# Row groups for depth-2 products, a re-cut wq gradient pass and an earlier second pass in a one-token transformer block's backward kernel

## The chip, the core and the metric

The kernel runs on one core of a Trainium2 chip. The metric is the device time of one execution in microseconds, from launch to end, as the median of 13 runs. The profile is of one execution; its span is counted from the first to the last instruction of the core.

## The reference, cut to what matters

The reference is the forward and the backward pass of one pre-norm block for a single decoded token: two batch rows (B=2), width D=640, 32 heads of depth 128, a cache of 4096 keys and values for each head, and a ReLU MLP of width 1728. All tensors are bfloat16.

```
h  = x + softmax(LN(x) wq  K^T * scale) V  wo
h2 = h + relu(LN(h) w1) w2
out_0 = h2
out_1..out_7 = gradients of x, k_cache, v_cache, wq, wo, w1, w2 for grad_out
```

Nearly all bytes belong to the caches. The gradients of K and V (out_2, out_3) are 64 tiles of 1 MB each, one for each pair of batch row and head. The four weight gradients out_4 (wq), out_5 (wo), out_6 (w1) and out_7 (w2) are outer products summed over the two batch rows, so each is a matrix product whose contraction has depth 2. The gradient of x also needs wq once more: the gradient of q times the transpose of wq.

## The kernel before, in words

**First pass.** `p1_iter(i)` (L373) is a software pipeline over the 64 (row, head) pairs. For pair i it transposes the K tile on TensorE (L327), lets ScalarE or VectorE copy the transposed groups from PSUM (L332, L330) and forms the scores (L338). For pair i-1 it computes the exponentials and the scaled keys `pk` on VectorE (L388). For pair i-2 it runs the sums over V and K (L381, L396). Its result is, for each pair, a matrix MT, two columns in OU (L489) and the probabilities P_bf.

**Middle.** `middle_gen(b)` (L609) is one generator for each batch row. It forms attention output, layer norm, MLP, and the gradient back to the output of attention. `go_group` (L566) then gives, for eight heads at a time, the gradient goc of each head's output: eight VectorE reductions (`ttr`, L552), a pair of matmuls `pr_ps` (L265) whose result goes to gom, and the matmuls `d_ps` (L581, L584) from which negdot and GQc, the gradient of q, come. `mlp_out(b)` (L593) computes and stores the block's output.

**Second pass.** `p2_iter(j)` (L688) takes pair j: it loads the V tile again (called Wt), transposes it as fp32 pairs (L348), multiplies with gom (L361), gets gsp (L696), and writes gradient tiles gK and gV by VectorE (two halves each, L683). GpSimd queues their stores (L721, L740). gK and gV share three buffers, and seven `ld` buffers hold K, V, W and the tiles of the last part.

**Last part.** `fin_gen` (L786) runs in the second pass's shadow. `rows_of` (L747) turns columns into rows with one small matmul per 128 values (L754) and a ScalarE copy (L756). `outer_rows` (L762) forms a weight gradient: each depth-2 matmul (L778, at most 512 columns) goes to one of three PSUM banks (`mid`, `m`, `a`) in turn, ScalarE copies it to an `ot` tile (L780), and GpSimd queues the store (L783). After the wo gradient and after all heads' GQc it reads wq in five tiles of 8 KB rows (L809), transposes them in groups of eight (L327, L332), and sums 32 heads into `gx_ps` (L822), which VectorE copies for each of five column blocks (L825). `ln_bwd`, two row stores and the wq gradient follow.

**What sets the order.** The kernel schedules by hand. A plan lists iterations: first-pass iteration i, with a second-pass pair j in every other one from `P2_AT` on, then second-pass pairs alone. Between the pipeline's steps, generators in two lists are advanced (`bg_step`): the middle with a credit of RATES per step, the last part with RATE2 per step; each yield costs what it states. `wait(n)` holds a generator back for some steps, `turn()` hands out slots for `ttr`, and `bg_until` forces the middle on at once when a pair j needs a head group that isn't ready. Loads are queued on SyncE in the order of a list (`pump`), as buffers come free. On each engine instructions run in the order in which they were emitted.

Of the kernel before, what the change touches and what calls it, by code (L numbers as in the profile page):

```python
# [7 lines left out]
FP32 = mybir.dt.float32  # L8
BF16 = mybir.dt.bfloat16
ALU = mybir.AluOpType  # L10
# [5 lines left out]
def kernel(  # L16
# [533 lines left out]
    def ttr(in0, in1, acc, width, kc=128):  # L550
        junk = cols.tile([128, D], BF16, tag="junk", name="junk")
        nc.vector.tensor_tensor_reduce(out=junk[0:kc, 0:width], in0=in0, in1=in1, scale=1.0, scalar=0.0,  # L552
                                       op0=ALU.mult, op1=ALU.add, accum_out=acc)
# [9 lines left out]
    def one(src, b):  # L563
        return src[:, :, b]

    def go_group(b, g, hbc):  # L566

        hs = slice(g * GH, (g + 1) * GH)
        go32 = small.tile([128, GH], FP32, tag="go32", bufs=1, name="go32")
        for k in range(GH):  # L570
            yield from turn()
            ttr(wo_t[:, g * GH + k, :], hbc[:], go32[:, k:k + 1], D)
            yield 0.9
        nc.vector.tensor_copy(out=goc[:, hs, b], in_=go32[:])
        pr = small.tile([128, GH], FP32, tag="pr", bufs=1, name="pr")
        nc.vector.tensor_tensor(out=pr[:], in0=goc[:, hs, b], in1=OU[:, b, hs, 0], op=ALU.mult)
        yield from wait(3)
        pair_rows(gom, goc, hs, slice(b, b + 1))
        yield from wait(2)
        d_ps = pst([128, 2, GH], FP32, "mid", "d_ps")  # L580
        nc.tensor.matmul(d_ps[:, 0, :], lhsT=ones_f32, rhs=pr[:], start=True, stop=True)  # L581
        for k in range(GH):
            h = g * GH + k
            nc.tensor.matmul(d_ps[:, 1, k:k + 1], lhsT=MTs.pop((b, h))[:], rhs=goc[:, h, b:b + 1],  # L584
                             start=True, stop=True)
        nc.vector.tensor_scalar(out=negdot[:, hs, b], in0=d_ps[:, 0, :], scalar1=-1.0, scalar2=None, op0=ALU.mult)
        ud = small.tile([128, GH], FP32, tag="ud", bufs=1, name="ud")
        nc.vector.tensor_tensor(out=ud[:], in0=OU[:, b, hs, 1], in1=negdot[:, hs, b], op=ALU.mult)
        nc.vector.tensor_tensor(out=ud[:], in0=d_ps[:, 1, :], in1=ud[:], op=ALU.add)
        nc.vector.tensor_scalar(out=GQc[:, hs, b], in0=ud[:], scalar1=SCALE, scalar2=None, op0=ALU.mult)  # L590
        yield ("go", b, g)

    def mlp_out(b):  # L593
        m_ps = pst([128, ND], FP32, "mid", "mlp_ps")
# [14 lines left out]
    def middle_gen(b):  # L609
# [47 lines left out]
        hbc = cols.tile([128, D], BF16, tag="rowbc", name="hbc")  # L657
        yield from bcast_cols(one(gh1c, b), ND, lambda c: 128, hbc)
        yield ("gh1", b)
        yield from go_group(b, 0, hbc)  # L660
        if b == 0:
            yield from mlp_out(b)
        for g in range(1, H // GH):
            yield from go_group(b, g, hbc)

    def ga_gen():

# [76 lines left out]

    fw = [0]

    def rows_of(pool, colsrc, n, total, name, tag):  # L747

        r = pool.tile([B, n * 128], BF16, tag=tag, bufs=2 if tag == "rD" else 1, name=name)
        for c0 in range(0, n, 4):  # L750
            cn = min(4, n - c0)
            t = pst([B, 512], FP32, "mid", "rw_ps")
            for k in range(cn):
                nc.tensor.matmul(t[:, k * 128:(k + 1) * 128], lhsT=colsrc[:, c0 + k, :], rhs=ident_bf[:],  # L754
                                 start=True, stop=True)
            nc.scalar.copy(out=r[:, c0 * 128:(c0 + cn) * 128], in_=t[:, 0:cn * 128])  # L756
            yield
        FIN[name] = r

    FIN = {}  # L760

    def outer_rows(pool, L, nrow, R, N, out_ap, cc):  # L762

        P = nrow // cc
        grp = max(1, min(cc, 4096 // N))
        out_v = out_ap.rearrange("(p c) n -> p c n", c=cc)
        for c0 in range(0, cc, grp):
            gn = min(grp, cc - c0)
            while free["ld"] < 1:
                yield  # L770
            ot = take("ld", [128, grp, N], "ot")
            for k in range(gn):
                n0 = 0
                while n0 < N:
                    nn = min(512, N - n0)
                    fw[0] += 1
                    o_ps = pst([128, 512], FP32, ("mid", "m", "a")[fw[0] % 3], "o_ps")
                    nc.tensor.matmul(o_ps[0:P, 0:nn], lhsT=L[:, bass.ds(c0 + k, P, step=cc)], rhs=R[:, n0:n0 + nn],  # L778
                                     start=True, stop=True)
                    nc.scalar.copy(out=ot[0:P, k, n0:n0 + nn], in_=o_ps[0:P, 0:nn])  # L780
                    n0 += nn
                    yield 0.55
            nc.gpsimd.dma_start(out=out_v[:, c0:c0 + gn, :], in_=ot[0:P, 0:gn, :])  # L783
            give(ot)

    def fin_gen(fin):  # L786
        yield from rows_of(fin, acol, NF, Dff, "ar", "rF")
        yield from rows_of(fin, gc, ND, D, "gr", "rD")
        yield from outer_rows(fin, FIN["ar"], Dff, FIN["gr"], D, out_7, Dff // 96)
        yield from rows_of(fin, ghfc, NF, Dff, "ghfr", "rF")  # L790
        yield from rows_of(fin, x2c, ND, D, "x2r", "rD")
        yield from outer_rows(fin, FIN["x2r"], D, FIN["ghfr"], Dff, out_6, ND)
        while ("gh1", B - 1) not in done:
            yield
        yield from rows_of(fin, OFc, H, HD, "OFr", "rH")
        yield from rows_of(fin, gh1c, ND, D, "gh1r", "rD")
        yield from outer_rows(fin, FIN["OFr"], HD, FIN["gh1r"], D, out_5, HD // 128)
        while ("go", 1, H // GH - 1) not in done:
            yield
        gx1 = fin.tile([128, B, ND], FP32, tag="gx1", name="gx1")  # L800
        wqn = A_wq.rearrange("(c p) n -> p c n", p=128)
        nxt = None
        for c in range(-1, ND):
            st = nxt
            if c + 1 < ND:
                while free["ld"] < 1:
                    yield
                nxt = take("ld", [128, NSC, 128], "wqs")
                nc.sync.dma_start(out=nxt[:], in_=wqn[:, c + 1, :].rearrange("p (h n) -> p h n", n=128))  # L809
            if c < 0:  # L810
                for _ in range(8):
                    yield
                continue
            acc = pst([128, B], FP32, "m", "gx_ps")
            for g in range(H // GT):
                t_sb = transpose_group(st, g)
                if g == H // GT - 1:
                    give(st)
                yield 0.9
                for j in range(GT):  # L820
                    h = g * GT + j
                    nc.tensor.matmul(acc[:], lhsT=t_sb[:, j, :], rhs=GQc[:, h, :],  # L822
                                     start=(h == 0), stop=(h == H - 1))
                yield
            nc.vector.tensor_copy(out=gx1[:, :, c], in_=acc[:])  # L825
        gx_bf = fin.tile([128, ND, B], BF16, tag="gxb", name="gx_bf")
        yield from ln_bwd(gx1[:], x1c[:], rstd1[:], gh1c[:], gx_bf[:], B)
        for b in range(B):
            gxo = small.tile([128, ND], BF16, tag="gxo", bufs=2, name="gxo")
            nc.vector.tensor_copy(out=gxo[:], in_=gx_bf[:, :, b])  # L830
            store_row(gxo[:], ND, out_1[b].rearrange("s (c p) -> (s c) p", p=128))
            yield
        yield from rows_of(fin, GQc, H, HD, "GQr", "rH")
        yield from rows_of(fin, x1c, ND, D, "x1r", "rD")
        yield from outer_rows(fin, FIN["x1r"], D, FIN["GQr"], HD, out_4, ND)


    bg = []
# [32 lines left out]
            assert bg and bg_one(bg) >= 0.0, mark  # L871
        forced[0] = False

    M0_ITERS = 12
    P2_AT = H + 2 + M0_ITERS
    RATES = (0.2, 0.6, 0.2, 0.8, 0.45)
    RATE2 = 0.68
    plan = []
    i = j = 0
    while i <= NP1 + 1 or j <= NP1:  # L880
# [58 lines left out]
    for n, (i, j) in enumerate(plan):  # L939
# [5 lines left out]
        if j is not None:  # L945
            while g2 is not None:
                p2_step()
            if j < NP1:
                bg_until(("go", j // H, (j % H) // GH))
            g2 = p2_iter(j, int(i is not None))  # L950
        reserve[0] = 2 if bg2 else 0
        if i is None and ("y", 1) in done and fin is None:
# [19 lines left out]
        for k, _ in enumerate(p1_iter(i, i < H + 1, int(H + 1 < i < P2_AT))):  # L972
            for _ in range(at.get(k, 0)):
                if g2 is not None:
                    p2_step()
            if k == 5:
                a_heads(i)
            pump()

            spread[0] = 1 if i < P2_AT else 2  # L980
            if i >= P2_AT:
                slot[0] = int(k == 6)
            elif i > H + 1:
                slot[0] = {1: 2, 4: 1, 6: 1}.get(k, 0)
            else:
                slot[0] = int(k in (1, 6))
            bg_step(0, rate)
            bg_step(1, RATE2)
# [38 lines left out]
```

## Time and profile before

| what | value |
|---|---|
| median of 13 runs | 1041.45 us (1034.02 to 1047.33) |
| the profiled execution | 1045.12 us |
| its span, first to last instruction | 1043.3 us |
| mean granted TensorE clock | 0.751 of full speed |
| moved by DMA | 221.48 MB read, 149.13 MB written, 355 GB/s over the span |
| weight loads of TensorE (PEld) | 745.6 us busy, 71% |
| VectorE / ScalarE | 654.3 us (63%) / 586.0 us (56%) |

The profile's page gives busy times of the engines, the span in 40 slices (each digit is a busy share in tenths; PEclk is the granted TensorE clock in tenths; DMA is the mean busy share of the core's 16 DMA engines), the chain of work that ended last, and groups of equal instructions with the idle time of the engine before them. A table of stretches gives the same for chosen stretches of time. Matmul ends are modelled, so a busy PE isn't PE at its peak. A DMA share can read slightly over 1.

### The profile page before, as it was taken

The page shows a single profiled execution, that of the slowest core. Times are in us where ns is not written, and L with a number is a line of the kernel's source. Part 1 is how long each engine was busy: PE and PEld are TensorE (multiplying, and loading weights), DVE is VectorE, ACT ScalarE, POOL GpSimd, SP SyncE. Part 2 cuts the span into 40 slices and gives each one's busy share as a digit, 9 for nine tenths or more (in the row PEclk, how much of TensorE's full clock was granted, in tenths as well). Part 3 has the DMA queues.
Part 4 walks back from the last instruction along what each step waited for, and adds up shares of the span by engine and source line. Part 5 has one row for each costly group of instructions (what it writes and reads, how often), then busy time and mean ns, then how long its engine had stood idle before and what let it go on. Part 6 is the DMA issues. An engine that isn't in the chain of part 4 may idle for free.

```text
span 1043.3 us, 30344 instructions
## 1 busy us (share of the span) xinstructions
PE 853.8 (82%) x13231; PEld 745.6 (71%) x13231; DVE 654.3 (63%) x1252; ACT 586.0 (56%) x1227; POOL 102.9 (10%) x220
## 2 busy tenths in 40 slices
PE   6999999999999998889896659898996465738971
PEld 5999999998888888878785547655666355625661
DVE  3545867755476575656586668675775675563556
ACT  4666656667675666656553336665663244626741
POOL 1000000000000000000011212121121111111212
PEclk9989989989797888978886555555556666865565
DMA  9999999998576498989899998998999999987998
GB/s 357 379 391 407 384 367 383 379 369 317 202 263 227 165 389 337 352 336 369 358 383 426 382 371 321 344 368 333 411 423 411 426 362 384 417 351 286 390 412 348
DMA packets 59748, 372.56 MB, mean 357 GB/s; under 512 B 5760, under 2 KB 15424, under 8 KB 17376
## 3 DMA queue, kind: packets, MB, share of 16 engines
q1 hardware_dynamic: 38960, 221.50, 56.0%
q0 software_dynamic: 20656, 149.14, 34.5%
q8 instruction: 103, 1.69, 0.6%
q14 instruction: 29, 0.24, 0.1%
HBM read 221.48 MB, written 149.13 MB: 355 GB/s over the span
## 4 chain that ended last, share of the span: by engine, by line
PE 56%; DMA 21%; ACT 8%; DVE 8%; issue 5%; POOL 0%; SPq 0%; POOLq 0%; DVEq 0%; ACTq 0%
PE t_ps L327 12%; PE m_ps L381 11%; PE t_ps L348 10%; DMA out_dram<-gK 8%; DMA Kt<-in_A_k_cache_dram 6%; DMA out_dram<-gV 6%; PE o_ps L778 4%; PE m_ps L396 4%; ACT t_sb L332 4%; DVE gV L683 4%; PE s_ps L338 4%; PE dp_ps L361 2%; DVE gK L683 2%; PE t_ps L319 2%; PE rw_ps L754 1%
## 5 line engine op out<-in xcount | busy, mean ns | idle before, releaser
L332 ACT COPY t_sb<-t_ps 128x1024 bf16<-128x1024 bf16 x243 | 239.7, 1014 | 86.7 <-PE t_ps L327 85.0
L348 PE MATMUL t_ps<-ident_f,Wt 128*128 128x128 f32 x1024 | 236.3, 380 | 0.8 <-ACT t_sb L332 0.5
L353 ACT COPY t_sb<-t_ps 128x512 f32<-128x512 f32 x256 | 149.2, 586 | 150.2 <-PE t_ps L348 147.2
L381 PE MATMUL m_ps<-pk,Vt 128*128 128x129 bf16 x2048 | 208.9, 232 | 1.9 <-issue 1.9
L348 PEld LDWEIGHTS t_ps<-ident_f,Wt 128*128 128x128 f32 x1024 | 167.6, 196 | 38.7 <-issue 19.7
L388 DVE TENSOR_TENSOR pk<-Kt,ep 128x2048 bf16<-128x2048 bf16 x128 | 156.2, 1220 | 48.6 <-ACT ep L438 46.3
L327 PE MATMUL t_ps<-ident_bf,Kt 128*128 128x128 bf16 x2048 | 167.2, 237 | 17.7 <-DMA Kt<-in_A_k_cache_dram 13.2
L683 DVE TENSOR_TENSOR gK<-rb,gsp 128x2048 bf16<-128x2048 bf16 x128 | 152.0, 1225 | 46.2 <-DMA out_dram<-gV 44.5
L683 DVE TENSOR_TENSOR gV<-rb,pp 128x2048 bf16<-128x2048 bf16 x128 | 152.4, 1219 | 42.2 <-DMA out_dram<-gK 32.1
L327 PEld LDWEIGHTS <-Kt 128*128 128x128 bf16 x2048 | 139.1, 107 | 23.7 <-DMA Kt<-in_A_k_cache_dram 14.5
L381 PEld LDWEIGHTS <-Vt 128*128 128x128 bf16 x2048 | 139.6, 105 | 9.0 <-issue 3.3
L361 PEld LDWEIGHTS <-t_sb 128*128 128x128 bf16 x2048 | 96.4, 107 | 54.3 <-ACT t_sb L353 31.8
L361 PE MATMUL dp_ps<-gom,t_sb 128*128 128x2 bf16 x2048 | 96.0, 168 | 21.6 <-ACT t_sb L353 20.9
L338 PE MATMUL s_ps<-qc,t_sb 128*128 128x1 bf16 x2048 | 89.8, 165 | 10.6 <-ACT t_sb L332 9.1
L338 PEld LDWEIGHTS <-t_sb 128*128 128x128 bf16 x2048 | 81.8, 99 | 15.7 <-ACT t_sb L332 13.4
L740 POOL DMA_DIRECT2D out_dram<-gV x64 | 34.2, 534 | 595.6 <-DVE gV L683 485.3
L780 ACT CAST ot<-o_ps 128x512 bf16<-128x512 f32 (+4 forms) x160 | 69.6, 484 | 13.1 <-PE o_ps L778 6.2
L696 DVE SCALAR_TENSOR_TENSOR gsp<-dp_ps,negdot,P_bf 128x64 bf16<-128x64 f32 x64 | 18.0, 281 | 74.3 <-PE dp_ps L361 74.1
L330 DVE COPY t_sb<-t_ps 128x1024 bf16<-128x1024 bf16 x33 | 22.8, 692 | 66.0 <-PE t_ps L327 66.0
L721 POOL DMA_DIRECT2D out_dram<-gK x64 | 34.0, 532 | 297.7 <-DVE gK L683 272.9
L396 PE MATMUL m_ps<-ep,Kt 128*128 128x1 bf16 x2048 | 61.6, 164 | 1.8 <-ACT OU L489 1.3
L488 ACT ACTIVATE MT<-m_ps,rtot 128x128 bf16<-128x128 f32 x64 | 23.5, 368 | 69.0 <-PE m_ps L381 69.0
(181 smaller groups left out, 858.7 us busy)
## 6 DMA issues: line engine op xcount, KB each, us to landing
Kt<-in_A_k_cache_dram SPq DMA_DIRECT2D x64, 1024.0 KB, 9.2
Vt<-in_A_v_cache_dram SPq DMA_DIRECT2D x64, 1024.0 KB, 7.4
Wt<-in_A_v_cache_dram SPq DMA_DIRECT2D x64, 1024.0 KB, 10.0
out_dram<-gV POOLq DMA_DIRECT2D x64, 1024.0 KB, 10.2
out_dram<-gK POOLq DMA_DIRECT2D x64, 1024.0 KB, 8.2
wo_t<-in_A_wo_dram SPq DMA_DIRECT2D x4, 1280.0 KB, 10.3
wqs<-in_A_wq_dram SPq DMA_DIRECT2D x5, 1024.0 KB, 7.8
out_dram<-ot POOLq DMA_DIRECT2D x5, 1024.0 KB, 10.5
```

Of the source, the lines that this page charges most:

```text
L327: nc.tensor.transpose(t_ps[:, j, :], nat[:, g * GT + j, :], ident_bf[:])
L332: nc.scalar.copy(out=t_sb[:], in_=t_ps[:])
L338: nc.tensor.matmul(dst[:, sc:sc + 1], lhsT=t_sb[:, j, :], rhs=vec, start=True, stop=True)
L348: nc.tensor.transpose(t_ps[:, j, :], natf[:, 2 * cc:2 * cc + 2, :].rearrange("p c k -> p (c k)"), ident_f[:])
L353: nc.scalar.copy(out=t_sb[:], in_=t_ps[:])
L361: nc.tensor.matmul(dst[:, sc:sc + 2], lhsT=v[:, j, :, par], rhs=vecs[:, par, :], start=(par == 0), stop=(par == 1))
L381: nc.tensor.matmul(r["m"][:, 0:129], lhsT=r["V"][:, sc, :], rhs=r["pk"][sc // HALF][:, sc % HALF, 0:129], start=False, stop=(sc == NSC - 1))
L388: nc.vector.tensor_tensor(out=p["pk"][k][:, :, 0:128].rearrange("p s (a two) -> p s a two", two=2), in0=p["K"][:, sl, :].rearrange("p s (a ...
L396: nc.tensor.matmul(r["m"][:, 129:130], lhsT=r["K"][:, sc, :], rhs=r["ep"][:, sc, 0:1], start=(sc == 0), stop=False)
L683: nc.vector.tensor_tensor(out=pairs_view(dst[:, sl, :]), in0=row.rearrange("p (a two) -> p a two", two=2)[:, None, :, :].to_broadcast([128 ...
L778: nc.tensor.matmul(o_ps[0:P, 0:nn], lhsT=L[:, bass.ds(c0 + k, P, step=cc)], rhs=R[:, n0:n0 + nn], start=True, stop=True)
L780: nc.scalar.copy(out=ot[0:P, k, n0:n0 + nn], in_=o_ps[0:P, 0:nn])
```

## The change

Four things are changed; the work that the reference asks for is the same.

1. **Weight gradients.** `rows_of` first spreads each column pair over the four 32-row groups (a ScalarE copy to a zeroed `wide` tile), so that the row vectors come out at partitions 0, 32, 64 and 96 of the row tile. `outer_rows` emits its depth-2 matmuls three at a time, each reading the operands of the next row group and writing another bank; the three ScalarE copies follow.
2. **wq gradient of x.** The pass over wq is cut by heads: six pieces of at most six heads ([128, 5, 768] tiles, rows of 1536 bytes), each summed over its heads in one `m` bank and added to `gx1` by VectorE. A piece runs between two tiles of the w1 or wo gradient as soon as its heads' GQc are there.
3. **Second pass sooner.** M0_ITERS goes from 12 to 10, so P2_AT goes from iteration 46 to 44. The first head group of row 0 is split in 2 and 6 heads, and `mlp_out(0)` comes after all of row 0's head groups.
4. **Rates.** RATE2 goes from 0.68 to 0.85, and one more `ttr` slot is given where an iteration has no pair j.

```diff
-    def go_group(b, g, hbc):
+    def go_group(b, h0, h1, hbc):
...
-        yield from go_group(b, 0, hbc)
+
+        bounds = (0, 2, 8, 16, 24, 32) if b == 0 else (0, 8, 16, 24, 32)
+        for h0, h1 in zip(bounds, bounds[1:]):
+            yield from go_group(b, h0, h1, hbc)
         if b == 0:
             yield from mlp_out(b)
-        for g in range(1, H // GH):
-            yield from go_group(b, g, hbc)
...
+            w = FIN["wide"][(c0 // 4) % 2]
+            nc.scalar.copy(out=w[:, 0:cn, :, 0:B], in_=col[:, c0:c0 + cn, None, :].to_broadcast([128, cn, 4, B]))
+            yield
+            yield
+            t = pst([128, 512], FP32, "mid", "rw_ps")
             for k in range(cn):
-                nc.tensor.matmul(t[:, k * 128:(k + 1) * 128], lhsT=colsrc[:, c0 + k, :], rhs=ident_bf[:],
-                                 start=True, stop=True)
+                nc.tensor.matmul(t[:, k * 128:(k + 1) * 128], lhsT=w[:, k, :, :].rearrange("p q x -> p (q x)"),
+                                 rhs=ident_bf[:], start=True, stop=True)
             nc.scalar.copy(out=r[:, c0 * 128:(c0 + cn) * 128], in_=t[:, 0:cn * 128])
-            yield
+            yield 0.7
...
+            todo = [(k, n0, min(512, N - n0)) for k in range(gn) for n0 in range(0, N, 512)]
+            for t0 in range(0, len(todo), 3):
+                part = []
+                for k, n0, nn in todo[t0:t0 + 3]:
+                    q = 32 * (fw[0] % 4)
+                    o_ps = pst([128, 512], FP32, ("mid", "m", "a")[len(part)], "o_ps")
+                    nc.tensor.matmul(o_ps[0:P, 0:nn], lhsT=L[q:q + B, bass.ds(c0 + k, P, step=cc)],
+                                     rhs=R[q:q + B, n0:n0 + nn], start=True, stop=True)
+                    part.append((o_ps, k, n0, nn))
                     fw[0] += 1
...
+                for o_ps, k, n0, nn in part:
                     nc.scalar.copy(out=ot[0:P, k, n0:n0 + nn], in_=o_ps[0:P, 0:nn])
-                    n0 += nn
-                    yield 0.55
+                yield 0.5 * len(part)
             nc.gpsimd.dma_start(out=out_v[:, c0:c0 + gn, :], in_=ot[0:P, 0:gn, :])
             give(ot)
+            if between is not None:
+                yield from between()
...
+        def gx_piece(k):
...
+            t = take("ld", [128, ND, QP * 128], "wqs")
+            nc.sync.dma_start(out=t[:, :, 0:hn * 128], in_=wq_r[:, :, k * QP * 128:(k * QP + hn) * 128])
+            yield from wait(6)
...
+                    if acc is None:
+                        acc = pst([128, ND, B], FP32, "m", "gx_ps")
+                    for x, (c, j) in enumerate(prev[1]):
+
+                        nc.tensor.matmul(acc[:, c, :], lhsT=prev[0][:, x, :], rhs=GQc[:, k * QP + j, :],
+                                         start=(c == 0 and j == 0), stop=(c == ND - 1 and j == hn - 1))
...
+            nc.vector.tensor_tensor(out=gx1[:], in0=gx1[:], in1=acc[:], op=ALU.add)
...
-    M0_ITERS = 12
+    M0_ITERS = 10
...
-    RATE2 = 0.68
+    RATE2 = 0.85
...
-                slot[0] = int(k == 6)
+                slot[0] = int(k == 6 or (k == 1 and j is None))
```

## The prediction, made before the changed kernel was run

> **What bounds the kernel now.** I read the page's engine rows and 40 slices first, then the table of stretches, the groups kept apart by shape, and the waits.
>
> ```profile
> PE 853.8 (82%) x13231; PEld 745.6 (71%) x13231; DVE 654.3 (63%) x1252; ACT 586.0 (56%) x1227; POOL 102.9 (10%) x220
> ...
> PEclk9989989989797888978886555555556666865565
> DMA  9999999998576498989899998998999999987998
> ```
>
> No engine is full over the whole span, but DMA is at 9 in most slices. The table of stretches (columns: length, then busy us of PE, PEld, DVE, ACT and POOL, granted clock, DMA share, GB/s) says where it isn't:
>
> ```profile
> 255.00:361.80 106.80, 98.67 (x1865) 90.31 (x1864) 65.24 (x180) 69.40 (x143) 0.00 (x0) 0.86 0.60 215
> 361.80:541.45 179.65, 157.34 (x2871) 146.61 (x2869) 116.05 (x223) 109.23 (x237) 13.61 (x27) 0.86 0.92 358
> 541.45:620.00 78.55, 48.37 (x636) 43.27 (x634) 52.15 (x91) 26.75 (x51) 12.71 (x27) 0.60 0.98 402
> 620.00:653.50 33.50, 30.06 (x260) 23.91 (x258) 28.18 (x45) 20.46 (x47) 6.48 (x14) 0.60 0.83 321
> 653.50:718.90 65.40, 56.86 (x410) 39.88 (x406) 39.28 (x66) 41.45 (x88) 10.44 (x23) 0.50 0.97 362
> 718.90:736.20 17.30, 16.52 (x127) 11.80 (x127) 14.71 (x25) 10.88 (x27) 3.16 (x8) 0.50 0.81 308
> 736.20:832.80 96.60, 73.54 (x659) 56.00 (x658) 65.02 (x105) 48.56 (x107) 16.83 (x35) 0.57 1.01 419
> 922.30:961.60 39.30, 27.77 (x206) 18.11 (x207) 19.97 (x23) 21.19 (x41) 6.33 (x15) 0.54 0.73 288
> ```
>
> The second pass alone (from 541) is a DMA stage, 402 to 419 GB/s at a share of 0.98 to 1.01. It has holes at 620-653, 718-736 and 922-961. In the first two PE is busy 90% and 95% at half clock: the depth-2 products of the weight gradients compete with the second pass's transposes. The stage 255-362, first pass beside the middle, is TensorE's (98.67 of 106.80 busy) with DMA at 0.60. The mixed stage (362-541) is mostly DMA's again.
>
> **The change, part by part.** *Products in row groups.* The groups by shape (count, then busy us and mean ns, then idle before) and a piece of PE's timeline:
>
> ```profile
> L778 PE MATMUL o_ps<-GQr,x1r 2*128 2x512 bf16 x40 | 20.2, 599 | 2.4 <-ACT ot L780 2.0 <-ACT x1r L756 0.3
> L780 ACT CAST ot<-o_ps 128x512 bf16<-128x512 f32 x87 | 48.9, 594 | 10.8 <-PE o_ps L778 4.0 <-DMA out_dram<-ot 2.3 <-PE dp_ps L361 1.0
> ```
>
> ```profile
> 644.53 0.40 PE L361 MATMUL dp_ps<-gom,t_sb 128*128 128x2 bf16 x8
> 644.86 1.52 PE L778 MATMUL o_ps<-gr,ar 2*96 2x128 bf16 x4
> ```
>
> Over its seven shapes L778 is 160 matmuls and 78.2 us (20.2+19.4+11.9+9.9+8.6+6.4+1.8), one after the other in each burst. In three row groups and three banks a full-width burst of three should take less than 3 x 599 = 1.80 us. The Trainium skill, "TensorE: Matmul & The Clock Gate", Part 3, gives 3.07 for four row tiles; at that efficiency (0.77) an estimate for three is 1.80/2.3 = 0.78 us. Against it stands "TensorEngine Tiling (Array Packing)", PSUM Bottleneck: tiling speeds TensorE, not the emptying of PSUM, and the copy may become the bound. The row makes that plain: one copy (594 ns) is as long as one matmul, three are 1.78 us, so by this rule a burst saves nothing. Which holds depends on who is full: over 939.33-998.92, the wq gradient's stage, the stretches give PE 55.43 of 59.59 us and ACT 41.48. ACT has 18 us to spare and PE none, so I take the saving: 40 matmuls in about 14 bursts save 20.2 - 14 x 0.78 = 9.3 us of PE there, and at the same ratio some 44 of all 78.
>
> That is PE time, not kernel time. It counts only in the DMA holes that PE makes: 620-653 is 33.5 x 0.17 = 5.7 us idle, of which the start of the last part is half: 2.5 back. 718.9-736.2: 17.3 x 0.19 = 3.3, 2 back. 653.5-718.9: 65.4 x 0.03 = 2, 1 back. 922.3-961.6: 39.3 x 0.27 = 10.6; the finer stretches put 3.9 before 939.3, a wait that stays (below), and 6.4 in 939.33-961.56, where PE is busy 21.20 of 22.23 us: 4.5 back. Sum -10 (bounds 0, if the bursts stay serial, and -17).
>
> *Spreading the rows.* 28 to 32 ScalarE copies of about 0.26 us (nearest row: pk<-ep, 260 ns) are 8 us of ACT, hidden by ACT's idle half; without that cover 8 us. The row matmuls keep their count, a 128-column weight load beside the 2-column one is 107 beside 109 ns. Two VectorE memsets: nothing. By the emitted order the last part still begins at pair 19 and ends at pair 57, so its tail moves nowhere, +0.
>
> *wq by pieces.* Transposes (160), copies (20) and `gx_ps` matmuls (160) keep their counts. The loads on SyncE move from pairs 43-49 to 31-49, ahead of W tiles, without more than one more `ld` buffer held. Rows shrink from 8 KB to 1536 bytes: the five 1024 KB loads land in 7.8 us (median), the 960 KB loads of the same form in the first pass in 10.2. If all of that were on the path it would be 5 x 2.4 = 12 us; a first-pass stretch that holds such a load (45-60) still moves 373 GB/s against 399 in the fullest one, 6%, or 0.9 us on 5.2 MB at 373. I take +1.5, nearer that row, bounds 0 to +12.
>
> A new wait comes with it: each piece ends with a VectorE add from bank `m`, and the next burst of products on `m` waits for it. VectorE, in order, may stand before the gK and gV halves that wait for stores. Before, such waits are:
>
> ```profile
> DVE gK L683 <- DMA out_dram<-gV: 44.5, 22, 6.6
> ...
> PE row_ps L545 <- DVE gxo L830: 11.6, 2, 11.3
> ...
> PE gx_ps L822 <- DVE gx L825: 9.8, 1, 9.8
> ```
>
> Queued behind the burst on PE are the transposes of W, and for them wait t_sb, gsp, gK and the store. But the stall arises while DMA has stores to do: the 9.8 us one lies in 865.6-883.0 at a share of 0.95, 0.9 us lost; one of 13.3 us (pr_ps for goc) in 832.8-846.6 at 0.89, 1.5 lost; the 11.3 one cost 3.9 (922.3-939.3 at 0.77). Six pieces at 0 to 3.9 are 0 to 23; most are followed by slack, so 0.5 each: +3.
>
> *Second pass sooner.* Iterations 44 and 45 of the first pass become a mixed pair. OU's starts give their cost: 324.88, 338.12, 348.23, so 13.24 + 10.11 = 23.4 us, against 7.08 for their neighbours. The reason is the clock:
>
> ```profile
> 324.00:327.50 3.50, 3.50 (x78) 3.11 (x74) 2.98 (x14) 2.45 (x4) 0.00 (x0) 1.00 0.57 169
> 327.50:331.00 3.50, 2.84 (x49) 2.49 (x49) 0.67 (x4) 0.02 (x1) 0.00 (x0) 0.62 1.01 382
> 331.00:334.50 3.50, 3.50 (x67) 3.40 (x64) 1.03 (x1) 1.83 (x5) 0.00 (x0) 0.50 0.19 75
> ```
>
> It halves just where `mlp_out(0)` waits (0.66 us) for the head group's VectorE tail, then issues 70 one-column matmuls, and stays so to 345. The skill's clock page, Part 1, ties a drop to some 3.4 us of idleness; no gap of that length is here, so the row decides that such a spot can drop the clock, and not that it always will. The change takes `mlp_out(0)` from this place; its 3.0 us of PE (1.16+1.20+0.65) go to the end of the mixed stage, covered by DMA (share 1.01 at 526-541), +1 for a part uncovered, +3 without cover. A mixed pair costs about 20.8 us (gV stores of pairs 1 to 6). So -23.4 + 20.8 + 1 here, and one pair fewer alone at the end: 3.15 MB at 419 GB/s = 7.5. Sum -9. If the drop comes all the same, its 9.2 us (23.35 - 14.15) stay and nearly nothing is left; without the MLP's part it could reach -11. By the emitted order the first two heads' `d_ps` stands a whole iteration ahead of pair 0, and heads 2 to 7 at pair 1, so nothing is forced.
>
> **Sum:** -10 + 0 + 1.5 + 3 - 9 = -14.5 us on the profiled 1045.12 (span 1043.3 and 1.8 around it). That execution lies 3.7 above the median of 1041.45; I take the sum off the median: 1027.
>
> **Rivals.** *The products' stage is DMA's anyway*: the bursts stay serial, or ACT's copies take over (three back to back hold up t_sb by 1.8 us), and only the sooner start counts: -9 + 1.5 + 1 = 1035. For it: 736-833 runs at 1.01 with the products in it. Against: 0.81 and 0.73 where PE is full. *Everything is regained*: -17 - 11 and no new waits, 1013; against: the gxo wait stays. *Slower*: the six adds behind stores. At the gxo wait's 3.9 each, 23 instead of 3, the sum is +6: 1047. It decides from 3 us each (gain gone) and is 0.3% slower from 3.5. For it: PE is in order and VectorE waits 76.6 us for stores (44.5 + 32.1 for gK and gV). Against: the two like stalls among pieces of work with slack cost 0.9 and 1.5.
>
> **Chances.** Forecast 0.50 (own range 1020 to 1034), DMA's anyway 0.22 (1030 to 1044), everything 0.12, slower 0.16. About 0.3% (3.1 us) is what can be told from no change. Faster: 0.50 + 0.12 + 0.14 of the second case = 0.76; same: 0.07 + 0.04 = 0.11; slower: 0.01 + 0.12 = 0.13. The range 1012 to 1045 leaves out 0.05 below and 0.11 above.
>
> **What would show it.** Products in bursts of three that overlap (about 0.8 us for three full-width ones) and fewer busy us on L778; DMA share over 0.9 in the stretches that were 0.83, 0.81 and 0.71; iterations around 44 without the half clock; PE waits for the add on gx under 3 us. I am wrong if bursts take 1.8 us, if the clock falls before pair 0 all the same, or if DMA shows holes after each wq piece.

## The result, and the profile after

The changed kernel takes 1021.25 us (median of 11 runs, 1016.05 to 1027.00); the kernel before, in the same sessions, 1041.48 us. The ratio is 0.983 (95% interval 0.980 to 0.985), about 18 us less. A second measurement gave 0.982 (0.978 to 0.986). Ratios use the fast runs alone, so they need not equal the quotient of the medians. The two profiled executions differ by more, 29 us (span 1043.3 and 1014.3), so below the ratios say how much and the profiles only where.

The page of the changed kernel: engine rows, then the granted clock and the DMA share in 40 slices.

```profile
PE 807.7 (80%) x13235; PEld 718.6 (71%) x13235; DVE 655.8 (65%) x1267; ACT 584.8 (58%) x1261; POOL 103.1 (10%) x220
...
PEclk9999999989799988988798557555675766556575
DMA  9999999999576899989999998999999999989998
```

The table of stretches of the changed kernel, at the same times as before except for the first, which ends sooner (columns: length, busy us of PE, PEld, DVE, ACT and POOL, granted clock, DMA share, GB/s):

```profile
255.00:325.00 70.00, 63.77 (x1263) 58.36 (x1262) 46.40 (x134) 47.56 (x99) 0.00 (x0) 0.90 0.61 221
620.00:653.50 33.50, 22.96 (x184) 17.00 (x184) 24.27 (x45) 18.82 (x49) 7.22 (x15) 0.54 0.87 338
653.50:718.90 65.40, 50.47 (x459) 39.81 (x458) 47.65 (x76) 41.96 (x102) 11.72 (x26) 0.53 1.01 390
718.90:736.20 17.30, 13.26 (x179) 11.99 (x178) 13.05 (x25) 9.45 (x15) 3.00 (x7) 0.73 1.01 409
736.20:832.80 96.60, 68.24 (x792) 54.02 (x791) 69.26 (x110) 54.46 (x108) 16.45 (x36) 0.67 1.02 421
922.30:961.60 39.30, 24.57 (x172) 14.28 (x171) 20.44 (x21) 23.40 (x48) 8.33 (x17) 0.51 0.99 382
```

PE (TensorE) is busy 46 us less, VectorE and ScalarE as long as before. At the times of the old holes the DMA share has risen: 0.83 became 0.87, 0.81 became 1.01, 0.73 became 0.99. Not all of that is a closed hole, since the work has moved: the wait for gxo, which lay in the third, now comes sooner, and 895 to 915 has a share of 0.76. Nothing here says which part of the change closed the others. The groups by shape and the waits (total us, times, longest) show three things that the prediction had named, the products' time on PE, the waits for the add on gx and the wait for gxo, and one that it had not:

```profile
L787 PE MATMUL o_ps<-GQr,x1r 2*128 2x512 bf16 x40 | 13.0, 575 | 9.7 <-ACT ot L792 9.5
L792 ACT CAST ot<-o_ps 128x512 bf16<-128x512 f32 x87 | 48.2, 608 | 27.2 <-DMA out_dram<-ot 23.5 <-PE o_ps L787 2.4
```

```profile
PE o_ps L787 <- DVE gx L841: 19.0, 5, 6.6
PE row_ps L545 <- DVE gxo L870: 10.8, 2, 10.4
```

The 40 largest products of the wq gradient cost PE 13.0 us instead of 20.2. But ScalarE's copies of this shape to `ot` now stand 23.5 us until earlier stores of `ot` have landed (2.3 before), and PE, in these products, 9.5 us behind such copies.

### The profile page after: what moved, and what is told of

Its sections match the earlier page's. It is cut to its first block, busy times and chain, and to the rows that moved or that the text cites. A ratio compares the mean times of both kernels' runs of the same rounds, so it can differ in the third digit from the quotient of the medians.

```text
span 1014.3 us, 30356 instructions
## 1 busy us (share of the span) xinstructions
PE 807.7 (80%) x13235; PEld 718.6 (71%) x13235; DVE 655.8 (65%) x1267; ACT 584.8 (58%) x1261; POOL 103.1 (10%) x220
## 4 chain that ended last, share of the span: by engine, by line
PE 45%; DMA 26%; ACT 9%; issue 9%; DVE 8%; POOL 1%; SPq 0%; POOLq 0%; DVEq 0%; ACTq 0%
PE m_ps L381 11%; PE t_ps L327 11%; DMA out_dram<-gK 8%; DMA Kt<-in_A_k_cache_dram 7%; PE t_ps L348 6%; DMA wqs<-in_A_wq_dram 4%; PE m_ps L396 4%; DVE gV L687 4%; PE s_ps L338 4%; DMA out_dram<-gV 3%; ACT t_sb L332 3%; DMA out_dram<-ot 3%; DVE gK L687 2%; PE t_ps L319 2%; PE dp_ps L361 2%
## 5 line engine op out<-in xcount | busy, mean ns | idle before, releaser
L332 ACT COPY t_sb<-t_ps 128x1024 bf16<-128x1024 bf16 x223 | 219.3, 1014 | 68.8 <-PE t_ps L327 67.5
L348 PE MATMUL t_ps<-ident_f,Wt 128*128 128x128 f32 x1024 | 225.1, 366 | 2.4 <-ACT t_sb L827 2.2
L381 PE MATMUL m_ps<-pk,Vt 128*128 128x129 bf16 x2048 | 206.1, 230 | 3.3 <-issue 3.1
L348 PEld LDWEIGHTS t_ps<-ident_f,Wt 128*128 128x128 f32 x1024 | 162.0, 190 | 36.6 <-issue 21.2
L327 PE MATMUL t_ps<-ident_bf,Kt 128*128 128x128 bf16 x2048 | 162.0, 232 | 16.4 <-DMA Kt<-in_A_k_cache_dram 14.3
L327 PEld LDWEIGHTS <-Kt 128*128 128x128 bf16 x2048 | 134.4, 104 | 21.4 <-DMA Kt<-in_A_k_cache_dram 15.6
L381 PEld LDWEIGHTS <-Vt 128*128 128x128 bf16 x2048 | 136.9, 104 | 10.5 <-issue 5.1
L361 PEld LDWEIGHTS <-t_sb 128*128 128x128 bf16 x2048 | 94.2, 106 | 55.4 <-ACT t_sb L353 44.2
L338 PEld LDWEIGHTS <-t_sb 128*128 128x128 bf16 x2048 | 81.1, 98 | 18.5 <-ACT t_sb L332 14.0
L488 ACT ACTIVATE MT<-m_ps,rtot 128x128 bf16<-128x128 f32 x64 | 23.5, 368 | 69.9 <-PE m_ps L381 66.7
L396 PEld LDWEIGHTS <-Kt 128*128 128x128 bf16 x2048 | 59.2, 97 | 1.7 <-issue 1.5
```

The lines of the kernel that those rows point to most:

```text
L327: nc.tensor.transpose(t_ps[:, j, :], nat[:, g * GT + j, :], ident_bf[:])
L332: nc.scalar.copy(out=t_sb[:], in_=t_ps[:])
L338: nc.tensor.matmul(dst[:, sc:sc + 1], lhsT=t_sb[:, j, :], rhs=vec, start=True, stop=True)
L348: nc.tensor.transpose(t_ps[:, j, :], natf[:, 2 * cc:2 * cc + 2, :].rearrange("p c k -> p (c k)"), ident_f[:])
L361: nc.tensor.matmul(dst[:, sc:sc + 2], lhsT=v[:, j, :, par], rhs=vecs[:, par, :], start=(par == 0), stop=(par == 1))
L381: nc.tensor.matmul(r["m"][:, 0:129], lhsT=r["V"][:, sc, :], rhs=r["pk"][sc // HALF][:, sc % HALF, 0:129], start=False, stop=(sc == NSC - 1))
```

## The experiments

Each kernel is compared with the kernel before in the same session. Part 1 of the change holds four things: another way of making rows, bursts of three, row groups, and (with part 4) a higher rate. So it was taken apart most.

| kernel | median us | ratio to before (95%) |
|---|---|---|
| changed kernel, first / second measurement | 1021.25 / 1024.43 | 0.983 (0.980 to 0.985) / 0.982 (0.978 to 0.986) |
| changed, products all in one row group, twice | 1015.92 / 1017.77 | 0.973 (0.968 to 0.979) / 0.976 (0.973 to 0.980) |
| changed, second pass at its old start | 1020.66 | 0.979 (0.974 to 0.984) |
| before + rate 0.85 | 1057.57 | 1.013 (1.010 to 1.017) |
| before + rate 0.85 + bursts in one row group | 1056.79 | 1.013 (1.009 to 1.017) |
| the same + new `rows_of` | 1029.18 | 0.983 (0.979 to 0.988) |
| the same + row groups | 1030.63 | 0.989 (0.984 to 0.993) |
| before + wq gradient of x by pieces | 1037.79 | 0.993 (0.990 to 0.995) |
| before + `mlp_out(0)` moved | 1041.67 | 0.999 (0.995 to 1.003) |
| changed, one row group, out_1's stores later | 1014.67 | 0.971 (0.966 to 0.976) |
| the same, second pass at its old start | 1015.70 | 0.970 (0.965 to 0.975) |

### Part 1 and its rate, on the kernel before

All of part 1 with RATE2 0.85; the wq pass, the start and `mlp_out` stay old.

```diff
-    def rows_of(pool, colsrc, n, total, name, tag):
+    def rows_of(pool, col, n, name, tag):
...
-    RATE2 = 0.68
+    RATE2 = 0.85
```

> The kernel before with the new rows and bursts in row groups and the rate 0.85, but the old start, the old place of mlp_out(0) and the old pass over wq at the end. If the last part's relief is worth the forecast's 10 us or more, 1028 to 1032; if row groups and rate do nothing because DMA bounds, 1039 to 1043.

It took 1030.63 us, ratio 0.989 (0.984 to 0.993): 12 us of the 18 are here. Which of its four things brings them, the next runs show.

### The products in one row group

The changed kernel, where each product reads partitions 0 and 1, so that all share one row group; the order of the instructions stays the same.

```diff
-                    q = 32 * (fw[0] % 4)
+                    q = 0
```

> The changed kernel with every depth-2 product in row group 0 again, in the same bursts of three on three banks; nothing else differs. If row groups are what relieves TensorE in the last part (the forecast's 10 us), bursts of three full-width products take about 1.8 us instead of 1.24 and the time rises by 5 to 10 us over the changed kernel's 1021, to 1026 to 1031. If that stage is DMA's anyway, and the spreading of the work did it, it stays within 3 us: 1018 to 1024.

It was not slower but faster, 0.973 (0.968 to 0.979), outside the changed kernel's interval. As the two had not been measured side by side, it was repeated beside the changed kernel on one chip:

> The changed kernel again, beside the one with row group 0 alone on the same chip. If row groups cost or save nothing, both come out within 0.4% of each other, near 0.98 of the kernel before; if the earlier distance (0.973 against 0.983) is the row groups', the changed kernel is about 1% slower again.

> The changed kernel with every product in row group 0, once more, as the partner of the run of the changed kernel. Forecast's theory: 5 to 10 us slower than it. Rival, that the last part is spread thinly enough for TensorE not to be short: equal within 4 us.

0.982 (0.978 to 0.986) with row groups, 0.976 (0.973 to 0.980) without. A third pair, the kernel with part 1 alone:

> The kernel with the old start and the old pass over wq, new rows, bursts and rate 0.85 (1030), now with every product in row group 0. There the products are packed into pairs 21 to 36 and 53 to 56. If row groups matter where the part is packed, 1038 to 1046; if bursts and the spacing of the rows are the gain, 1026 to 1034.

0.983 (0.979 to 0.988) against 0.989 (0.984 to 0.993). The two of this pair were on different chips, and the intervals of the last two pairs overlap, but all three point the same way: row groups cost 0.5 to 1%.

They do what they say on PE. PE's timeline, two bursts of three full-width products of the w1 gradient, first of the changed kernel, then of the one with a single row group (columns: start, duration, what; in brackets the idle time before it):

```profile
666.09 0.62 PE L787 MATMUL o_ps<-ghfr,x2r 2*128 2x512 bf16 x3
677.66 0.84 PE L787 MATMUL o_ps<-ghfr,x2r 2*128 2x512 bf16 x3 [0.67 <-ACT ot L792]
```

```profile
657.92 1.47 PE L787 MATMUL o_ps<-ghfr,x2r 2*128 2x512 bf16 x3
671.11 1.44 PE L787 MATMUL o_ps<-ghfr,x2r 2*128 2x512 bf16 x3 [0.51 <-ACT ot L792]
```

All four ran at half clock. The first burst of each kernel waited for nothing: 0.62 us, as long as one such product alone, against 1.47. The second came after a wait for ScalarE, and the gain is smaller, 0.84 against 1.44; after the longest such wait in the wq gradient's products (7.7 us, in the other kernel 5.8) the burst took 1.56 us in both. Over the last part the union of all products' busy time is 45.9 us with row groups, 61.5 without, 69.5 before. Those 15.6 us of PE bring nothing. The waits between 605 and 665, changed kernel first (total us, times, longest):

```profile
PE o_ps L787 <- ACT ot L792: 10.2, 4, 8.6
ACT ot L792 <- DMA out_dram<-ot: 9.6, 1, 9.6
```

```profile
ACT ot L792 <- DMA out_dram<-ot: 3.3, 1, 3.3
...
PE o_ps L787 <- ACT ot L792: 2.7, 3, 1.7
```

and what goes with that, two stretches of the table, again first with row groups:

```profile
635.00:645.00 10.00, 1.35 (x6) 0.96 (x5) 5.86 (x11) 1.51 (x5) 1.82 (x4) 0.50 1.01 414
645.00:655.00 10.00, 7.91 (x63) 6.10 (x62) 5.08 (x11) 6.88 (x18) 1.29 (x3) 0.50 0.82 307
```

```profile
635.00:645.00 10.00, 8.01 (x62) 6.45 (x61) 4.22 (x9) 7.04 (x19) 1.59 (x4) 0.50 1.01 416
645.00:655.00 10.00, 7.54 (x71) 6.55 (x70) 6.51 (x9) 6.18 (x16) 1.54 (x4) 0.50 1.01 347
```

With row groups ScalarE reaches the next `ot` tile early, stands 9.6 us before its store, and PE, in order, stands behind it with the transposes of W queued (1.35 us busy of 10). DMA is full meanwhile, and ten microseconds later it has a hole (0.82): the stores that PE should have prepared are missing. In the profiles of the second pair ScalarE's longest such wait is 8.0 against 1.7 us. By the times at which GpSimd queues the gV stores, the single row group gains 3.4 us here in the first pair (its lead goes from 5.1 at pair 22 to 8.5 at pair 23) and 3.0 in the second (6.2 to 9.2). The rest of its lead in these profiles, over 4 us, was there before the first product, so it is not the row groups'. No kernel with more `ot` buffers was run, so this reading of the loss is from traces, not shown by experiment.

### The rate alone, bursts, and the new rows

> The kernel before with one number changed, the last part's rate 0.85 instead of 0.68 (10 to 11 single products a pair instead of 8 to 9, out of pairs 20 to 32). If the rate is what the rows-and-bursts kernel gained by, about 1030; if more products a pair on a full TensorE at half clock only deepen the holes, 1041 to 1050.

```diff
-    RATE2 = 0.68
+    RATE2 = 0.85
```

1057.57 us, 1.013 (1.010 to 1.017): the rate by itself costs 14 us. To it the bursts were added, all in row group 0, with the old `rows_of`:

```diff
+            todo = [(k, n0, min(512, N - n0)) for k in range(gn) for n0 in range(0, N, 512)]
+            for t0 in range(0, len(todo), 3):
...
+                    q = 0
```

> The kernel with the rate 0.85 alone (1057) plus bursts of three in row group 0, with the old rows (no spreading copies, so the part stays packed into pairs 20 to 31 and 51 to 54). If emitting three products at once is what helps, 1030 to 1040; if it is the looser spacing that the new rows bring, 1050 to 1058.

1.013 (1.009 to 1.017), on another chip than the rate alone: bursts, with their slightly lower charge (0.5 credits for a product instead of 0.55), are worth nothing that can be told. Between this and 0.983, measured in the same session, lies only the new `rows_of` with its zeroed tiles and one wait of four steps. Stretches of the table between the same pairs, counted by gV stores (19 to 23, 23 to 27, and part of 50 to 57), old rows first:

```profile
620.80:657.00 36.20, 34.44 (x258) 27.26 (x256) 27.56 (x46) 24.91 (x60) 6.82 (x16) 0.55 0.83 306
657.00:708.10 51.10, 42.05 (x305) 27.92 (x304) 26.31 (x41) 33.35 (x71) 7.31 (x16) 0.50 0.84 332
925.00:965.00 40.00, 33.31 (x209) 18.90 (x208) 14.74 (x15) 26.54 (x52) 6.04 (x13) 0.50 0.69 272
```

```profile
628.20:656.20 28.00, 26.76 (x219) 22.07 (x220) 27.40 (x46) 20.49 (x52) 6.37 (x13) 0.56 0.91 353
656.20:697.10 40.90, 34.68 (x283) 24.85 (x282) 26.34 (x41) 26.67 (x65) 6.81 (x16) 0.58 1.01 388
913.50:946.00 32.50, 29.24 (x255) 19.29 (x252) 19.77 (x20) 25.76 (x57) 8.21 (x16) 0.66 0.97 391
```

Four pairs take 36.2 us against 28.0, the next four 51.1 against 40.9, and pairs 50 to 57 80.1 against 65.1; at the very end the old rows are ahead (34.1 against 39.3). Each time the slower kernel is the one whose DMA has holes: 0.83, 0.84 and 0.69 against 0.91, 1.01 and 0.97.

A chunk of rows costs 0.5 credits in the old form, 1.7 in the new (two yields and 0.7), and there are 32 chunks. So at a rate of 0.85 the old rows bunch the last part: 32 row matmuls between two gV stores, products in pairs 20 to 31 and 51 to 54; with the new rows at most 20, and products in pairs 21 to 36 and 52 to 56. The bunch of row matmuls alone is not what the rate brought, for the kernel before has one of 33; its products, though, run on for some five pairs longer. PE's timeline of the kernel with the rate alone shows the bunch:

```profile
701.29 0.58 PE L754 MATMUL rw_ps<-ident_bf,OFc 128*2 128x128 bf16 x4 [0.66 <-ACT OFr L756]
702.54 0.58 PE L754 MATMUL rw_ps<-ident_bf,OFc 128*2 128x128 bf16 x4 [0.66 <-ACT OFr L756]
703.78 0.58 PE L754 MATMUL rw_ps<-ident_bf,OFc 128*2 128x128 bf16 x4 [0.66 <-ACT OFr L756]
705.03 0.58 PE L754 MATMUL rw_ps<-ident_bf,gh1c 128*2 128x128 bf16 x4 [0.66 <-ACT OFr L756]
```

Five chunks, the first at 700.04, follow each other with nothing between them, and before each of the four shown PE stands 0.66 us for ScalarE to empty the one bank. That wait is not the difference itself: between 600 and 760 PE's waits before row matmuls sum to 10.0 us in the kernel with old rows and bursts and to 8.4 with the new, where 5.5 of them are for the `wide` copy. What differs is what lies between the chunks. Whether it is the pauses alone, or the form of the matmul (128 output partitions instead of 2) too, no run separates; nor was the new `rows_of` run at the old rate of 0.68.

### The wq gradient of x by pieces

The pieces on the kernel before, with rate 0.68, single products and the old start.

```diff
-        yield from outer_rows(fin, FIN["ar"], Dff, FIN["gr"], D, out_7, Dff // 96)
...
+            nc.vector.tensor_tensor(out=gx1[:], in0=gx1[:], in1=acc[:], op=ALU.add)
...
+                yield from gx_ready()
```

> The kernel before with one part of the change: the wq gradient of x in six pieces between the tiles of the w1 and wo gradients, rate 0.68, single products, old start. Products then run from pair 20 to 49 instead of 20 to 36. If spreading is the gain, 1028 to 1034; if the pieces' waits behind stores cost what the slower rival said, 1045 or more; if TensorE's product time is the whole matter, 1038 to 1043.

1037.79 us, 0.993 (0.990 to 0.995): 7.7 us faster, not slower. Its waits for the add are longer than in the changed kernel. The first view below is a line of the waits, the second the table of stretches where they lie:

```profile
PE o_ps L778 <- DVE gx L826: 41.9, 5, 10.5
```

```profile
720.00:780.00 60.00, 48.74 (x550) 39.23 (x551) 47.63 (x79) 35.95 (x69) 10.44 (x23) 0.66 1.00 402
780.00:840.00 60.00, 40.30 (x449) 31.79 (x448) 43.83 (x73) 29.97 (x62) 12.79 (x24) 0.66 1.02 423
840.00:900.00 60.00, 36.45 (x460) 29.11 (x459) 33.70 (x39) 29.76 (x57) 9.44 (x21) 0.70 1.01 414
```

Five waits of 8.4 us on average, and DMA at 1.00 to 1.02 all the time: there was other traffic to move, and PE had slack. In the kernel before, the same three stretches read:

```profile
720.00:780.00 60.00, 58.28 (x433) 40.00 (x432) 46.25 (x76) 39.92 (x96) 11.48 (x24) 0.50 0.95 388
780.00:840.00 60.00, 31.14 (x345) 27.35 (x344) 38.67 (x63) 18.42 (x36) 9.03 (x19) 0.61 1.00 416
840.00:900.00 60.00, 41.06 (x585) 36.87 (x584) 35.08 (x46) 31.49 (x47) 9.62 (x21) 0.68 0.97 380
```

PE 58 of 60 us busy, then 31, then 41, with DMA at 0.95, 1.00 and 0.97. With the pieces put between the tiles of products, these spread from pairs 20 to 36 over pairs 20 to 49; PE is below 49 of 60 and DMA is full. That the spreading is the gain is a reading of these two profiles: the largest difference, 414 GB/s against 380, lies from 840 to 900, where the kernel before runs its pass over wq with its wait of 9.8 us, and no run separates the two.

### The earlier start, and the clock

Two runs: the changed kernel with the old start, and the kernel before with only `mlp_out(0)` moved behind row 0's head groups.

```diff
-    M0_ITERS = 10
+    M0_ITERS = 12
```

> The changed kernel with the second pass beginning at iteration 46 as before; mlp_out(0) stays in its new place. If the gain of this part is the earlier start itself (one pair fewer alone at the end), the time rises by some 9 us, to 1030. If it is the avoided half clock at mlp_out(0), the two iterations cost 14 us instead of 20.8 for the mixed pair, the lost pair 7.5, and the time stays within 2 us of the changed kernel's: 1019 to 1023.

```diff
-        yield from go_group(b, 0, hbc)
+        for g in range(0, H // GH):
+            yield from go_group(b, g, hbc)
         if b == 0:
             yield from mlp_out(b)
-        for g in range(1, H // GH):
-            yield from go_group(b, g, hbc)
```

> The kernel before with one edit: mlp_out(0) after all head groups of row 0. If its 70 one-column matmuls drop the clock, iterations 44 and 45 go from 23.4 to about 14.2 us and the time falls by 9, to 1032. If the clock falls at this place for another reason, or the time is given back to the DMA stage later, it stays at 1041 within 3.

The start is worth nothing: 0.979 (0.974 to 0.984) with the old one, 0.982 and 0.983 with the new. Nor is the place of `mlp_out(0)`: 0.999 (0.995 to 1.003). Yet the clock behaved as read. The stretches of the kernel with `mlp_out(0)` moved, where the kernel before fell to 0.62 and 0.50:

```profile
327.50:331.00 3.50, 3.03 (x59) 2.82 (x58) 3.33 (x9) 2.71 (x7) 0.00 (x0) 1.00 0.96 360
331.00:334.50 3.50, 3.50 (x84) 3.19 (x85) 3.46 (x11) 2.44 (x4) 0.00 (x0) 1.00 0.11 40
```

Iterations 44 and 45 take 14.7 us instead of 23.4. In the six profiles with the old start and `mlp_out(0)` in its old place they take 21.2 to 23.4, in the three with the old start and it moved 14.5 to 14.7. But the drop can come at the new place instead: in this kernel `mlp_out(0)` now starts at 517.8, and from 519.6 to 536.4 the clock is 0.50, PE busy 15.97 of 16.80 us and the DMA share 0.81; in the changed kernel with the old start the same happens from 495.1 to 512.0 (PE busy throughout, DMA 0.85). By the times at which GpSimd queues the gV stores, the kernel with it moved leads the kernel before by 8.2 us at pair 0, 10.5 at pair 6, 6.9 at pair 10, 4.9 at pair 19 and 0.7 at pair 25, and lags by 3.5 at pair 36. So some of the lead goes in the stretch where the clock now falls. The rest swings: it is 5.6 again at pair 31, and this profile ends 5.7 us ahead, though the medians are equal. These are single profiles; what takes the lead isn't settled.

### A faster version

The hole that the prediction expected to stay, the two waits for gxo, is still there. In a kernel with one row group, the two stores of out_1 were put after the rows of GQ.

```diff
-            store_row(gxo[:], ND, out_1[b].rearrange("s (c p) -> (s c) p", p=128))
-            yield
+            gxos.append(gxo)
         yield from rows_of(fin, GQc, H, "GQr", "rH")
+        for b in range(B):
+            store_row(gxos[b][:], ND, out_1[b].rearrange("s (c p) -> (s c) p", p=128))
+            yield
```

> The changed kernel with row group 0 alone (1016 to 1018) and the two row stores of the gradient of x moved behind the rows of GQ, so that TensorE no longer stands at row_ps until VectorE, behind the stores, has made gxo (10.4 us, share of DMA 0.74 to 0.78 there). If that hole is DMA time lost, 3 to 5 us less: 1012 to 1014. If DMA catches up, no change: 1015 to 1019.

> The same as the run beside it, with the second pass beginning at iteration 46 as in the kernel before. If the earlier start is worth nothing once mlp_out(0) has moved, the two are within 4 us of each other; if it is worth the forecast's 9, this one is at 1021 to 1026.

The changed kernel's stretch with the hole, then that of the new kernel between the same gV stores, and a line of the new kernel's waits:

```profile
895.00:915.00 20.00, 8.14 (x103) 7.08 (x104) 10.42 (x14) 7.19 (x19) 2.65 (x7) 0.64 0.76 299
```

```profile
897.70:917.70 20.00, 9.72 (x110) 8.86 (x108) 12.29 (x14) 8.38 (x20) 3.87 (x8) 0.59 0.97 408
```

```profile
PE row_ps L545 <- DVE orow L547: 11.6, 1, 11.6
```

The share in this stretch rises (0.76 to 0.97), but the wait is not gone. The first out_1 row goes through after 0.7 us; for the second PE stands 11.6 us, from 908.7 to 920.3, until VectorE has copied the first (`orow`), and the 12.3 us after 917.7 have a share of 0.83 (0.92 after 915.0 in the changed kernel). So the hole is smaller and later. The time, 1014.67 us and 0.971 (0.966 to 0.976), can't be told from 0.973 and 0.976 without that edit. With the old start it is 0.970 (0.965 to 0.975). Both are faster than the kernel before and than the changed one, and the single row group is enough for that, as 0.973 and 0.976 show.

## Why the prediction was right, and where its steps failed

The direction and nearly the size were right: 14.5 us less were forecast, 18 came. The sum was right by errors that cancel, so its nearness is luck. Measured one by one, part 1 with its rate gives 0.989, the pieces 0.993, `mlp_out` 0.999; 0.989 x 0.993 x 0.999 = 0.981, against 0.982 and 0.983 measured (0.979 with the old start).

**Products in row groups, -10: failed as to kernel time.** The bursts overlap as forecast where no bank is waited for (0.62 us against 1.47, a factor of 2.4); there the estimate of 2.3 from the Trainium skill's "TensorE: Matmul & The Clock Gate", Part 3, agrees with the trace. After a wait for ScalarE the factor was 1.7 (0.84 against 1.44) or 1 (1.56 in both). The forecast's saving of 44 us on PE was too large; 23.6 us were saved in all (69.5 to 45.9), 15.6 of them by the row groups. Its base was too long, because 599 ns is a matmul's duration and not its share of a burst: three in one row group take 1.44 to 1.47 us, not 1.80. And 44 is not "the same ratio": 9.3 of 20.2 us gives 36 of 78. Neither figure went into the -10. The step that failed is "DMA holes that PE makes": PE's time for products was not what was missing there, since the kernels with one row group have 15.6 us more of it and are faster. Three pairs of kernels say that row groups add 0.5 to 1%. The rule that spoke against, "TensorEngine Tiling (Array Packing)", PSUM Bottleneck, has the better of it in time: a burst saved nothing at the end. But what held up the work behind ScalarE's copies was, by the trace, less their length than the `ot` store.

**Spreading the rows, +0: failed, the largest term.** The copies are hidden as said (about 0.23 us each; ScalarE is busy 584.8 us against 586.0). But the step looked only at their cost and at the emitted ends, pair 19 and pair 57, not at how the work lies between them. The new `rows_of` is worth 3% at rate 0.85 (1.013 to 0.983); what in it does that, its pauses or its form, stays open. And the rate was given no term at all; alone it costs 1.3%.

**wq by pieces, +1.5 and +3: failed in sign.** Measured -7.7 us on the kernel before. The loads in short rows land in 22.7 us (median) instead of 7.8, but DMA moves 409 to 421 GB/s from 718.9 to 832.8, where most of them run, so no loss of rate shows. They run at another place than the old ones, beside the products' stores; whether the place or the short rows make them land later, no run separates. The new wait came, larger than assumed, and no loss shows for it. That the work between the products would be worth more than it costs was not in the sum.

**Second pass sooner, -9: right in the trace, 0 in time.** The clock's drop goes with `mlp_out(0)`'s place; with `mlp_out(0)` alone moved the lead is 8.2 us at pair 0 and 0.7 at pair 25, and the medians are equal. The step treated a lead in front of a DMA stage as if the end moved with it. It also took the moved piece as covered, and in two kernels the clock fell there too. (Its mixed pair is a little too cheap: the gV stores of pairs 1 to 6 are 21.2 us apart in the trace, not 20.8.)

**The rivals.** *DMA's anyway* was right that row groups bring nothing, wrong that the sooner start counts and that the rest is nothing. *Slower* named its deciding point: 3 us for each add. The changed kernel's are 3.8 each (19.0 in 5), the pieces' alone 8.4, and both kernels are faster: it is refuted. The reason that the prediction gave for the smaller figure, that the stall comes while DMA has stores to do, fits the share of 1.00 to 1.02 beside these waits. *Everything regained*, 1013, is near the best version (1014.67), but by other means. The gxo wait stays, as said (10.4 us at the longest).

Three of the four signs that were to be seen came, one of them not in full: bursts of 0.62 and 0.84 us, DMA over 0.9 in two of three stretches (0.87 in the other), no half clock around iteration 44. The fourth, waits for gx under 3 us, did not (6.6 at the longest). Two of the signs that came belong to steps that gained nothing: a sign that an edit does its work isn't yet one that the work counts.

## What to carry to other kernels

Where background work runs beside a DMA-bound stage, how it lies there can matter more than its cost: here the higher rate alone lost 1.3%, and with slower rows on top of it the kernel was 3% faster than that, 1.7% faster than before. Before crediting a saving on an engine to the end, ask what that engine reaches sooner, and whether the buffer it needs there is free: when an engine works in order, an early arrival blocks all that stands behind it (8.6 us of PE here). A large wait need cost nothing as long as the bound resource has a backlog (five of 8.4 us, with DMA at 1.00 to 1.02), so weigh waits by the DMA share in the stretch where they lie.

## What the runs showed of the hardware

- Three depth-2 products of 512 columns at half clock (0.50 in that stretch) take 1.47 us in one row group and 0.62 us in three where no output bank is waited for; after a wait for ScalarE, 1.44 and 0.84.
- The clock halved near 328 us without a long idle gap: PE waited 0.66 us and then began 70 one-column matmuls, and the clock fell 0.2 to 1.3 us after the first of them. All six profiles with that piece in its old place and the old start show this, none of the three with it moved; in two of these three the clock halved for 17 us at the piece's new place. Whether the wait or the matmuls do it, no run separates.
- A 960 KB load in rows of 1536 bytes took 22.7 us (median) from issue to landing in the midst of stores, while DMA as a whole kept 409 to 421 GB/s. The old loads, 1024 KB in rows of 8 KB and at another place, took 7.8 us.
